# Channel attention and gated convolution on one core: taps decoded earlier, second load in two pieces, casts and transposes re-bound

## The chip, the core and the metric

The kernel runs on one core of one Trainium2 chip. The core's engines work side by side, each through its own instructions in order: TensorE (PE, with the loading of its weights shown apart as PEld), VectorE (DVE), ScalarE (ACT), GpSimd (POOL) and SyncE (SP), which issues most of the loads. The metric is the device time of one execution in microseconds (us); lower is better. It is given as the median of several runs.

## The reference

`q`, `k`, `v` are 4 x 6336 x 256 in float32 (a batch of 4, 6336 rows, 256 channels). The first half is attention over channels, the second a gated causal convolution with five taps:

```python
qn = q / (norm(q, axis=1) + 1e-6);  kn = k / (norm(k, axis=1) + 1e-6)
s = kn.transpose(0, 2, 1) @ qn / tau                 # 4 x 256 x 256
a = softmax(s)                                       # over the last axis
x = v @ a                                            # 4 x 6336 x 256
gate = sigmoid(sum_k conv_w[k] * x[:, row - 4 + k])  # five taps, causal
out = (gate * (x @ w_val)) @ w_out
```

The norms run over the 6336 rows, so a batch's scores, and with them all of its second half, are known only when all of its rows of `q` and `k` have been seen.

## The kernel before

**Two passes for each batch.** The first pass walks over `q` and `k` in 17 groups of up to 3 x 128 rows (group 0 has two such rows of 128, group 3 two and a rest of 64). A group is loaded by `load_group` (line 78) into one of six `raw` buffers, one DMA for its q and one for its k. `score_group` (line 239) adds its part to the scores: some rows go through TensorE in float32 as they are (`s_ps<-raw`), others are split into a rounded part and a remainder (`hi`: ACT's cast on line 269, POOL's subtraction on line 270) and take three faster products (`s_ps<-hi`). The squares for the norms are made on ACT (`sq`, line 288, three buffers) and added up partly on DVE in PSUM (`acc_ps`, line 293), partly on POOL (`acc`). In the first batch's groups 0 to 3 all rows go raw; from group 4 on two rows go raw and one is split. Batch 1 has raw rows only in its groups 0 to 3, and after that everything is split.

`softmax` (line 328) is a generator; each `tick` runs one stage of it: sum of both accumulators (`acc_all`, line 337), column sums on TensorE (line 342), roots, reciprocals, exponentials, `a`. Then `a` is transposed (line 395, `o_ps<-ident,a`), copied by ACT (`at`, line 399) and multiplied with w_val (line 404).

The second pass walks over `v` in 13 steps of up to 508 rows. Per step: `transpose_v` (line 436) turns `v` on TensorE (`t_ps`) and splits it (ACT line 446, DVE line 447); `conv` makes x (`x_ps`) and the tap sums (ACT line 469, DVE line 471); `sigmoid` (line 474) runs on ACT; `value` multiplies x @ w_val in (DVE line 489); `split_g` splits the product into `g_hi` (ACT line 502) and `g_lo` (POOL line 503); `finish` (line 506) multiplies by w_out (`o_ps`, line 519) and stores.

**Interleaving.** The second pass of batch b is interleaved with the first pass of batch b+1: the last loop (line 691) runs per step the steps of the one and as many groups of the other as `due_after` asks for. `split_group` issues a group's cast, squares and additions, `run_group` its products. Only batch 0's first pass runs alone.

**Inputs in 64 bits.** The weights and the taps come as 64-bit floats and are decoded with integer operations on DVE (`decode`, `decode_past`), w_val and the taps (`wk`, 10 x 128, ten operations on lines 152 to 166, 204, 206) during batch 0's first pass. The raw words of w_val lie in one of the three `hi` buffers until then.

**What sets the order.** A scheduler orders each engine's instructions after the order of the program text, priorities (`high_priority` around the softmax stages) and explicit bindings: `behind("KEY")` makes what is issued inside wait in the order, not in time, until after the instruction last marked with that key. Marks used here: `SIG` the sigmoid, `ACT` the last copy of an output pair or of a softmax stage, `VH` the cast of v, `GH` the cast to `g_hi`, `SCORES` the last score product. PSUM tiles with the tag `bank` share four banks: `o_ps`, `t_ps`, `val_ps`, the softmax's and `warm`; a tile waits until the one that had its bank has been read.

Of the kernel before, what the change touches and what calls it, by code (L numbers as in the profile page):

```python
# [17 lines left out]
P = 128  # L18
# [6 lines left out]
EARLY = 2  # L25
# [6 lines left out]
def kernel(  # L32
# [45 lines left out]
    def load_group(b, g):  # L78
        j0, n = groups[g]
        t = raw_p.tile([P, 2, GROUP, C], F32, name="raw")  # L80
        for s, src in ((0, q), (1, k)):
            main = src[b, 0:RP * P].rearrange("(p j) c -> p j c", j=RP)
            last_load[0] = nc.sync.dma_start(out=t[:, s, 0:n, :], in_=main[:, j0:j0 + n, :])  # L83
            if rest_of(g):
                nc.sync.dma_start(out=t[0:REST, s, n, :], in_=src[b, RP * P:N])
        raws[b, g] = t
# [152 lines left out]
    def score_group(b, g):  # L239
# [58 lines left out]
        with tc.issue_after(cast.ins) if cast else nullcontext():  # L298
            if owed:
                owed.pop()()  # L300
            if b == 1 and LEAD <= g < LEAD + OWE:
                owed.append(norms)
            elif not late:
                norms()
# [18 lines left out]
        if late:  # L323
            later.append(norms)
        return ([clear] if g == 0 else []) + [lambda np_=np_, j=j: mms(np_, j) for np_, j0, nj in parts for j in range(j0, j0 + nj)]


    def softmax(b):
# [64 lines left out]
        for h in range(NH):  # L393
            for h2 in range(NH):
                nc.tensor.transpose(at_ps[:, (h2 * NH + h) * P:(h2 * NH + h + 1) * P],
                                    a[:, h, h2 * P:(h2 + 1) * P], ident)
        yield
# [108 lines left out]
    def finish(b, i):  # L506
# [5 lines left out]
        for j in range(0, nt, 2):  # L512
            pair = offs[j:j + 2]
            o_ps = ps.tile([P, 512], F32, name="o_ps", tag="bank")
            for u, off in enumerate(pair):
                n_ = 0
                for h in range(NH):
                    for gs, ws in ((gh, wo_hi), (gh, wo_lo), (gl, wo_hi)):
                        nc.tensor.matmul(o_ps[:, u * C:(u + 1) * C], gs[:, h, off:off + P], ws[:, h, :],  # L519
                                         start=n_ == 0, stop=n_ == 3 * NH - 1)  # L520
                        n_ += 1
            if (b, i) == all_steps[-1]:

                for u, (copy, dma) in enumerate(((nc.scalar.copy, nc.scalar), (nc.vector.tensor_copy, nc.sync))[:len(pair)]):
                    copy(o_sb[:, j + u, :], o_ps[:, u * C:(u + 1) * C])
                    first = max((j + u) * P - pair[u], 0)
                    dma.dma_start(out=out[b, t0 + pair[u] + first:t0 + pair[u] + P], in_=o_sb[first:P, j + u, :])
                continue
# [62 lines left out]
    for n in range(NG):  # L591
        if n == 1:
            load_taps()
            load_weights(0)
            for _ in prepare_weights(2):
                pass
            prep.append(prepare_weights(0))
        if n == NG - 4:
# [7 lines left out]
        with behind(*(["SPIN"] if n < 2 else [])):  # L606
            run_group()
        if n == 0:
            with behind("SCORES"):
                spin(4)  # L610
        if n == 9:
# [79 lines left out]
    for n in range(len(all_steps)):  # L691
# [3 lines left out]
        turns = due_after(n) - (issued - len(ready))  # L695
        if n == 0:
            sigmoid(*now)
        for turn in range(turns):
            if turn == 0:
                run_group()  # L700
                with behind(*(["ACT", "VH", "SIG"] if n < EARLY else ["ACT"])):
                    split_group()
# [24 lines left out]
        if new:  # L727
            for h in range(NH):
                transpose_v(*new, h)
        tick()  # L730
# [36 lines left out]
```

## Time and profile before

| What | Value |
|---|---|
| median of 3 runs | 649.9 us (649.16 to 649.97) |
| profiled execution, its own time | 649.27 us |
| its span, first to last instruction | 647.4 us |
| PE busy | 635.9 us, 98% of the span |
| DVE, ACT, POOL busy | 523.4, 470.9, 391.3 us |
| mean granted TensorE clock | 0.995 of full speed |
| loaded and stored | 79.11 MB and 25.95 MB |

A row of the timeline reads: start, duration, engine, line, operation, output tile <- input tiles, sizes, number of merged instructions, and in square brackets the idle time of the engine before it and what ended it. "SPq" and "ACTq" are the sequencers that issue DMAs. Rows of equal instructions are merged, and durations of PE overlap (the ends of matmuls are modelled), so distances are read from start to start. PEclk is the granted clock, 1.00 is full speed.

### The profile page before, as it was taken

The page shows a single profiled execution, that of the slowest core. Times are in us where ns is not written, and L with a number is a line of the kernel's source. Part 1 is how long each engine was busy: PE and PEld are TensorE (multiplying, and loading weights), DVE is VectorE, ACT ScalarE, POOL GpSimd, SP SyncE. Part 2 cuts the span into 40 slices and gives each one's busy share as a digit, 9 for nine tenths or more (in the row PEclk, how much of TensorE's full clock was granted, in tenths as well). Part 3 has the DMA queues.
Part 4 walks back from the last instruction along what each step waited for, and adds up shares of the span by engine and source line. Part 5 has one row for each costly group of instructions (what it writes and reads, how often), then busy time and mean ns, then how long its engine had stood idle before and what let it go on. Part 6 is the DMA issues. An engine that isn't in the chain of part 4 may idle for free.

```text
span 647.4 us, 10814 instructions
## 1 busy us (share of the span) xinstructions
PE 635.9 (98%) x4051; PEld 573.0 (89%) x4051; DVE 523.4 (81%) x826; ACT 470.9 (73%) x620; POOL 391.3 (60%) x205
## 2 busy tenths in 40 slices
PE   9999999999999999999999999999999999999996
PEld 7888889999888999999998989999998898888886
DVE  4999798787787878878787869777878889888884
ACT  5677797858787697778788688778679565655564
POOL 2784599768655598859765559686775222212221
PEclk9989999999999999999999999999999999999998
DMA  8989665455434556545543546552322343343213
GB/s 299 402 294 347 207 230 172 151 191 184 128 118 146 196 177 207 181 147 174 166 159 99 190 154 223 189 170 66 97 80 67 123 132 110 106 131 107 64 41 111
DMA packets 73674, 105.77 MB, mean 163 GB/s; under 512 B 4300, under 2 KB 55702, under 8 KB 73622
## 3 DMA queue, kind: packets, MB, share of 16 engines
q1 hardware_dynamic: 47846, 79.76, 37.0%
q10 hardware_dynamic: 25776, 25.32, 12.5%
q8 instruction: 32, 0.52, 0.3%
q14 instruction: 20, 0.16, 0.1%
HBM read 79.11 MB, written 25.95 MB: 162 GB/s over the span
## 4 chain that ended last, share of the span: by engine, by line
PE 86%; DVE 5%; ACT 3%; POOL 2%; issue 1%; DMA 1%; SPq 1%; ACTq 0%; POOLq 0%
PE o_ps L519 21%; PE x_ps L455 20%; PE s_ps L316 19%; PE val_ps L455 19%; PE t_ps L445 6%; DVE gate L471 2%; DMA raw<-in_k_dram 1%; POOL hi L270 1%; PE o_ps L404 1%; DVE acc_ps L293 1%; SPq L83 0%; ACT L477 0%; ACT L375 0%; ACT sq L288 0%; POOL g_lo L503 0%
## 5 line engine op out<-in xcount | busy, mean ns | idle before, releaser
L471 DVE SCALAR_TENSOR_TENSOR gate<-x_ps,cw,gate 128x508 f32<-128x508 f32 (+1 forms) x416 | 276.6, 720 | 12.6 <-ACT gate L469 10.6
L270 POOL TENSOR_TENSOR hi<-raw,hi 128x1536 fp32r<-128x1536 f32 (+3 forms) x62 | 180.3, 2911 | 81.7 <-ACT hi L269 81.7
L503 POOL TENSOR_TENSOR g_lo<-gate,g_hi 128x1016 fp32r<-128x1016 f32 (+1 forms) x50 | 116.2, 2324 | 110.2 <-ACT g_hi L502 101.1
L293 DVE TENSOR_TENSOR acc_ps<-acc_ps,sq 128x512 f32<-128x512 f32 (+1 forms) x135 | 94.1, 697 | 71.0 <-ACT sq L288 68.6
L455 PE MATMUL x_ps<-v_hi,w 128*128 128x512 f32 (+1 forms) x416 | 140.2, 394 | 0.9 <-DVE rz L379 0.9
L316 PE MATMUL s_ps<-hi 128*128 128x256 f32 (+1 forms) x912 | 131.6, 289 | 2.8 <-POOL hi L270 2.6
L455 PE MATMUL val_ps<-v_hi,w 128*128 128x508 f32 (+1 forms) x416 | 133.8, 383 | 0.0
L316 PEld LDWEIGHTS s_ps<-hi 128*128 128x128 f32 (+1 forms) x912 | 118.6, 191 | 7.7 <-POOL hi L270 3.6
L529 ACT COPY o_sb<-o_ps 128x512 f32<-128x512 f32 x99 | 58.2, 588 | 78.3 <-PE o_ps L519 78.1
L519 PE MATMUL o_ps<-wo_hi,g_hi 128*128 128x256 f32 x400 | 113.3, 283 | 1.3 <-ACT at L399 1.3
L519 PE MATMUL o_ps<-wo_hi,g_lo 128*128 128x256 f32 x400 | 112.3, 281 | 0.0
L519 PE MATMUL o_ps<-wo_lo,g_hi 128*128 128x256 f32 x400 | 112.2, 281 | 0.0
L288 ACT ACTIVATE sq<-raw 128x1536 f32<-128x1536 f32 (+2 forms) x72 | 96.0, 1342 | 4.9 <-DVE acc_ps L293 3.9
L455 PEld LDWEIGHTS x_ps<-v_hi,w 128*128 128x128 f32 x416 | 77.4, 188 | 15.3 <-ACT z L377 1.3
L455 PEld LDWEIGHTS val_ps<-v_hi,w 128*128 128x128 f32 x416 | 77.1, 188 | 13.6
L293 POOL TENSOR_TENSOR acc<-acc,sq 128x512 f32<-128x512 f32 x57 | 74.5, 1306 | 23.2 <-ACT sq L288 23.0
L469 ACT ACTIVATE gate<-x_ps,cw 128x508 f32<-128x508 f32 (+1 forms) x104 | 68.4, 670 | 20.8 <-PE x_ps L455 20.2
L269 ACT CAST hi<-raw 128x1536 fp32r<-128x1536 f32 (+3 forms) x62 | 76.8, 1241 | 5.7 <-PE s_ps L316 2.0
L446 ACT CAST v_hi<-t_ps 128x512 fp32r<-128x512 f32 (+1 forms) x104 | 56.1, 567 | 33.9 <-PE t_ps L445 31.3
L455 PE MATMUL x_ps<-v_lo,w 128*128 128x512 f32 (+1 forms) x208 | 79.6, 382 | 0.0
L455 PE MATMUL val_ps<-v_lo,w 128*128 128x508 f32 (+1 forms) x208 | 79.1, 380 | 0.0
L489 DVE TENSOR_TENSOR gate<-val_ps,gate 128x508 f32<-128x508 f32 (+1 forms) x104 | 64.1, 658 | 17.4 <-ACT gate L477 17.2
(114 smaller groups left out, 819.4 us busy)
## 6 DMA issues: line engine op xcount, KB each, us to landing
raw<-in_q_dram SPq DMA_DIRECT2D x60, 384.0 KB
raw<-in_k_dram SPq DMA_DIRECT2D x60, 384.0 KB
v_raw<-in_v_dram SPq DMA_DIRECT2D x44, 512.0 KB
out_dram<-o_sb ACTq DMA_DIRECT2D x47, 384.0 KB
out_dram<-o_sb ACTq DMA_DIRECT2D x47, 124.0 KB
raw<-in_q_dram SPq DMA_DIRECT2D x8, 256.0 KB
raw<-in_k_dram SPq DMA_DIRECT2D x8, 256.0 KB
v_raw<-in_v_dram SPq DMA_DIRECT2D x4, 384.0 KB
```

The costliest lines, as they stand in the source:

```text
L269: cast = nc.scalar.copy(hi[r, js, :, 0, :], rows_of[r, js])
L270: nc.gpsimd.tensor_tensor(hi[r, js, :, 1, :], rows_of[r, js], hi[r, js, :, 0, :].bitcast(F32), ALU.subtract)
L288: nc.scalar.activation(sq[0:np_, ja:jb], rows_of[0:np_, ja:jb], AF.Square)
L293: add = eng.tensor_tensor(st[key][0:np_], st[key][0:np_], sq[0:np_, j], ALU.add)
L316: marks["SCORES"] = nc.tensor.matmul(st["s"][:, h, :], lhs, rhs, start=False, stop=stop and h == NH - 1 and n_ == len(ops) - 1)
L455: marks["PRODUCT"] = nc.tensor.matmul(ps, wt[:, which, ws, ch, hs], vs[:, ch, lo:hi_], start=ws == 0 and ch == 0 and vs is th, stop=ws == ...
L469: marks["TAP"] = nc.scalar.activation(gate[:, h, 0:w], x_ps[:, 0:w], AF.Copy, scale=cw[:, h:h + 1])
L471: marks["GATE"] = nc.vector.scalar_tensor_tensor(gate[:, h, 0:w], x_ps[:, tap:tap + w], cw[:, tap * NH + h:tap * NH + h + 1], gate[:, h, 0 ...
L489: nc.vector.tensor_tensor(gate[:, h, 0:w], vals[h][:, 0:w], gate[:, h, 0:w], ALU.mult)
L503: nc.gpsimd.tensor_tensor(gl[:, :, 0:w], gate[:, :, 0:w], gh[:, :, 0:w].bitcast(F32), ALU.subtract)
L519: nc.tensor.matmul(o_ps[:, u * C:(u + 1) * C], gs[:, h, off:off + P], ws[:, h, :], start=n_ == 0, stop=n_ == 3 * NH - 1)
L529: marks["ACT"] = nc.scalar.copy(o_sb[:, j:j + len(pair), :], o_ps[:, 0:len(pair) * C].rearrange("p (j c) -> p j c", c=C))
```

## The change

1. `load_group`: group 1 of batch 0 is loaded in two pieces, row block 0 first (q and k), then blocks 1 and 2. Its product list gets a `pause` of two dummy products (`spin(2)`) after the first row block; the four dummy products after group 0 are gone.
2. The taps (and tau) are loaded ahead of group 3 instead of behind group 4, and their ten decoding operations are issued at n == 0 instead of n == 1. w_val's load stays where it was.
3. The sigmoid of step 0 is issued after the step's first `run_group`, and in step 0 the cast of the next group is no longer bound behind it; the squares that batch 1's groups 4 to 6 owe to a later turn are bound behind the last sigmoid instead. From the third step on (`n >= EARLY`) a step's first cast is bound behind `GH`, the cast to `g_hi`, too.
4. The last transpose of `a` is marked `AT`, and the transposes of `v` are issued behind it.
5. In the very last step the two halves of the output pair go to two PSUM banks instead of one.

```diff
@@ load_group
-        for s, src in ((0, q), (1, k)):
-            main = src[b, 0:RP * P].rearrange("(p j) c -> p j c", j=RP)
-            last_load[0] = nc.sync.dma_start(out=t[:, s, 0:n, :], in_=main[:, j0:j0 + n, :])
-            if rest_of(g):
-                nc.sync.dma_start(out=t[0:REST, s, n, :], in_=src[b, RP * P:N])
+        for ja, jb in ((0, 1), (1, n)) if (b, g) == (0, 1) else ((0, n),):
+            for s, src in ((0, q), (1, k)):
+                main = src[b, 0:RP * P].rearrange("(p j) c -> p j c", j=RP)
+                last_load[0] = nc.sync.dma_start(out=t[:, s, ja:jb, :], in_=main[:, j0 + ja:j0 + jb, :])
+                if rest_of(g):
+                    nc.sync.dma_start(out=t[0:REST, s, n, :], in_=src[b, RP * P:N])
@@ score_group
             if owed:
-                owed.pop()()
+                with behind("SIG"):
+                    owed.pop()()
...
-        return ([clear] if g == 0 else []) + [lambda np_=np_, j=j: mms(np_, j) for np_, j0, nj in parts for j in range(j0, j0 + nj)]
+        def pause():
+            with behind("SCORES"):
+                spin(2)
+
+        products = ([clear] if g == 0 else []) + [lambda np_=np_, j=j: mms(np_, j) for np_, j0, nj in parts for j in range(j0, j0 + nj)]
+        if (b, g) == (0, 1):
+            products.insert(1, pause)
+        return products
@@ softmax
-                nc.tensor.transpose(at_ps[:, (h2 * NH + h) * P:(h2 * NH + h + 1) * P],
-                                    a[:, h, h2 * P:(h2 + 1) * P], ident)
+                marks["AT"] = nc.tensor.transpose(at_ps[:, (h2 * NH + h) * P:(h2 * NH + h + 1) * P],
+                                                  a[:, h, h2 * P:(h2 + 1) * P], ident)
@@ finish
             pair = offs[j:j + 2]
+            last = (b, i) == all_steps[-1]
             o_ps = ps.tile([P, 512], F32, name="o_ps", tag="bank")
+            halves = [o_ps, ps.tile([P, 512], F32, name="o_ps", tag="bank") if last and len(pair) > 1 else o_ps]
             for u, off in enumerate(pair):
                 n_ = 0
+                o_ps = halves[u]
...
-                    copy(o_sb[:, j + u, :], o_ps[:, u * C:(u + 1) * C])
+                    copy(o_sb[:, j + u, :], halves[u][:, u * C:(u + 1) * C])
@@ the loops
     for n in range(NG):
-        if n == 1:
+        if n == 0:
             load_taps()
-            load_weights(0)
             for _ in prepare_weights(2):
                 pass
+        if n == 1:
+            load_weights(0)
             prep.append(prepare_weights(0))
...
-        if n == 0:
-            with behind("SCORES"):
-                spin(4)
...
-        if n == 0:
-            sigmoid(*now)
         for turn in range(turns):
             if turn == 0:
                 run_group()
-                with behind(*(["ACT", "VH", "SIG"] if n < EARLY else ["ACT"])):
+                if n == 0:
+                    sigmoid(*now)
+                with behind(*(["ACT", "VH"] + ["SIG"] * (n > 0) if n < EARLY else ["ACT", "GH"])):
                     split_group()
...
         if new:
-            for h in range(NH):
-                transpose_v(*new, h)
+            with behind("AT"):
+                for h in range(NH):
+                    transpose_v(*new, h)
```

The order of POOL's instructions stays the same throughout; on the other engines the change reads as follows at three places. The line numbers of the changed kernel are a few higher.

The first place is DVE in batch 0's first pass, from the first addition of squares (`acc_ps<-acc_ps,sq`; `wk` are the taps, `bits` belongs to w_val). Before:

```order
L293 TENSOR_TENSOR acc_ps<-acc_ps,sq 128x512 x7
L152 TENSOR_SCALAR wk<-wk_raw 10x128
L293 TENSOR_TENSOR acc_ps<-acc_ps,sq 64x512
L154 SCALAR_TENSOR_TENSOR wk_raw<-wk_raw,wk 10x128
L176 TENSOR_SCALAR bits<-w_raw 128x512
L156 TENSOR_SCALAR wk<-wk_raw 10x128
L293 TENSOR_TENSOR acc_ps<-acc_ps,sq 128x512
L158 TENSOR_SCALAR wk<-wk 10x128
L293 TENSOR_TENSOR acc_ps<-acc_ps,sq 128x512
L178 SCALAR_TENSOR_TENSOR w_raw<-w_raw,bits 128x512
L160 TENSOR_SCALAR wk<-wk 10x128
L162 SCALAR_TENSOR_TENSOR wk<-wk_raw,wk 10x128
```

and now:

```order
L294 TENSOR_TENSOR acc_ps<-acc_ps,sq 128x512 x2
L153 TENSOR_SCALAR wk<-wk_raw 10x128
L294 TENSOR_TENSOR acc_ps<-acc_ps,sq 128x512
L155 SCALAR_TENSOR_TENSOR wk_raw<-wk_raw,wk 10x128
L157 TENSOR_SCALAR wk<-wk_raw 10x128
L159 TENSOR_SCALAR wk<-wk 10x128
L294 TENSOR_TENSOR acc_ps<-acc_ps,sq 128x512
L161 TENSOR_SCALAR wk<-wk 10x128
L294 TENSOR_TENSOR acc_ps<-acc_ps,sq 128x512
L163 SCALAR_TENSOR_TENSOR wk<-wk_raw,wk 10x128
L294 TENSOR_TENSOR acc_ps<-acc_ps,sq 128x512
L165 TENSOR_SCALAR wk_raw<-wk_raw 10x128
```

The first taps operation has moved from behind the seventh addition to behind the second, and the rest now stand singly or in threes between the additions of groups 1 to 3; the run of four without an addition (lines 162 to 204), which stood before group 5's additions, is gone.

The second place is ACT at the start of the second pass of batch 0, from the cast of batch 1's group 4 to the cast to `g_hi` of step 0. Before:

```order
L269 CAST hi<-raw 128x6x256
L446 CAST v_hi<-t_ps 128x512 x2
L477 ACT_TABLE_LOAD
L477 ACTIVATE gate<-gate 128x1016
L269 CAST hi<-raw 128x6x256
L288 ACTIVATE sq<-raw 128x1536
L446 CAST v_hi<-t_ps 128x512
```

and now:

```order
L270 CAST hi<-raw 128x6x256
L455 CAST v_hi<-t_ps 128x512 x2
L270 CAST hi<-raw 128x6x256
L486 ACT_TABLE_LOAD
L486 ACTIVATE gate<-gate 128x1016
L289 ACTIVATE sq<-raw 128x1536
L455 CAST v_hi<-t_ps 128x512
```

The cast of group 5 has moved ahead of the sigmoid and its table load.

The third place is TensorE in the softmax of batch 2, and the same again in batches 1 and 3 (`a` is the attention matrix, `v_raw` the next step's v). Before:

```order
L455 MATMUL x_ps<-v_hi,w 128x512
L395 MATMUL o_ps<-ident,a 128x128 x2
L445 MATMUL t_ps<-ident,v_raw 128x128 x4
L395 MATMUL o_ps<-ident,a 128x128 x2
L445 MATMUL t_ps<-ident,v_raw 128x128 x4
L519 MATMUL o_ps<-wo_hi,g_hi 128x256
```

and now:

```order
L464 MATMUL x_ps<-v_hi,w 128x512
L404 MATMUL o_ps<-ident,a 128x128 x4
L454 MATMUL t_ps<-ident,v_raw 128x128 x8
L531 MATMUL o_ps<-wo_hi,g_hi 128x256
L531 MATMUL o_ps<-wo_lo,g_hi 128x256
```

All of `a` is transposed ahead of `v`; on ACT the copy to `at` has accordingly moved ahead of both casts of `v` (it stood between them).

## The prediction

> **What bounds the kernel now.** I read the page first, then the waits of TensorE, then its timeline around each wait, and last what the releaser had been doing.
>
> ```profile
> span 647.4 us, 10814 instructions
> ```
>
> PE is busy for 98% of this span (first part of the page, in the table above), so only the few places where it waits or runs slowly can give time back. The waits name them (us in total, times, longest):
>
> ```profile
> PE s_ps L316 <- POOL hi L270: 2.6, 2, 1.4
> PE o_ps L519 <- ACT at L399: 1.3, 2, 1.0
> ```
>
> The first row's two waits are in batch 0's first pass and early in its second pass; the second row's are in the softmaxes of batches 1 and 2. The granted clock is read from windows of the first pass (the columns are PE, PEld, DVE, ACT and POOL busy, PEclk, DMA share, GB/s):
>
> ```profile
> 29.62:33.03 3.41, 2.04 (x13) 1.54 (x12) 3.34 (x6) 2.74 (x3) 3.41 (x4) 1.00 1.03 401
> 33.03:36.44 3.41, 3.41 (x9) 2.70 (x10) 3.34 (x6) 2.55 (x3) 3.41 (x3) 0.50 0.85 331
> 84.23:87.64 3.41, 2.41 (x15) 1.80 (x13) 3.41 (x7) 3.41 (x4) 3.41 (x2) 1.00 0.34 113
> ```
>
> After a window in which PE was busy for 2.04 of 3.41 us, the next 3.41 us were granted half the clock. A window with 2.41 us busy had no such sequel.
>
> **Part 1: the taps on DVE.** TensorE's timeline around that place:
>
> ```profile
> 28.39 1.89 PE L316 MATMUL s_ps<-raw 128*128 128x256 f32 x8
> ...
> 31.76 0.85 PE L316 MATMUL s_ps<-hi 128*128 128x256 f32 x5 [1.37 <-POOL hi L270]
> 32.54 0.38 PE L233 MATMUL tau_ps<-tau_sb,ones 1*128 1x1 f32 x2
> 32.85 3.64 PE L316 MATMUL s_ps<-raw 128*128 128x256 f32 x8
> ...
> 37.08 1.89 PE L316 MATMUL s_ps<-raw 128*128 128x256 f32 x8
> ...
> 39.51 1.89 PE L316 MATMUL s_ps<-raw 128*128 128x256 f32 x8
> ```
>
> An undisturbed group takes 39.51 - 37.08 = 2.43 us. The group from 28.39 took 32.85 - 28.39 = 4.46; less 2.43 and tau's 0.31 (32.54 to 32.85) the wait cost 1.7. The group at half clock took 37.08 - 32.85 = 4.23, so the slow clock cost 1.8. Why was POOL late?
>
> ```profile
> 11.61 1.27 POOL L293 TENSOR_TENSOR acc<-acc,sq 128x512 f32<-128x512 f32 x1 [10.11 <-ACT sq L288]
> ...
> 14.46 0.20 DVE L152 TENSOR_SCALAR wk<-wk_raw 10x128 int32<-10x128 int32 x1
> 14.96 1.28 POOL L270 TENSOR_TENSOR hi<-raw,hi 128x512 fp32r<-128x512 f32 x1 [2.08 <-ACT hi L269]
> ...
> 20.90 1.27 POOL L270 TENSOR_TENSOR hi<-raw,hi 128x512 fp32r<-128x512 f32 x1
> 21.05 1.27 DVE L162 SCALAR_TENSOR_TENSOR wk<-wk_raw,wk 10x128 int32<-10x128 int32 x1
> ...
> 26.86 0.68 DVE L293 TENSOR_TENSOR acc_ps<-acc_ps,sq 128x512 f32<-128x512 f32 x1
> ...
> 27.57 1.49 ACT L288 ACTIVATE sq<-raw 128x1536 f32<-128x1536 f32 x1 [3.20 <-DVE acc_ps L293]
> 28.97 0.60 ACT L269 CAST hi<-raw 128x512 fp32r<-128x512 f32 x1
> ...
> 29.37 0.69 DVE L182 TENSOR_SCALAR bits<-bits 128x512 int32<-128x512 int32 x1
> ...
> 30.45 1.26 POOL L270 TENSOR_TENSOR hi<-raw,hi 128x512 fp32r<-128x512 f32 x1
> ```
>
> A taps operation alone takes 0.20 us; one that meets a POOL instruction ends just behind it (22.32 against 22.17) and so takes up to 1.27. Four such in a row held group 5's additions back to 27.54. With three `sq` buffers group 8's squares had to wait for these, group 9's cast stood behind the squares on ACT, POOL's subtraction behind the cast, and PE behind that.
>
> In the new order the taps run from about 10.2 us on, since their load now stands right behind group 2's k (landed by 10.04, ACT's row below). I add up DVE's new order from there, additions at 0.70, taps operations at 0.3 where POOL is idle (by its two rows until 11.61 and from 12.88 to 14.96) and at POOL's next end where it is not. Depending on who wins two close races, group 4's additions end at 22.4 or 23.7 us, group 5's at 24.4 or 25.7, and the operation of row 29.37 at 27.0 or 28.3. Group 8's squares then start by 25.7, group 9's cast by 27.2, POOL's addition and subtraction end by 29.8. PE, some 0.4 us earlier than now (part 2), wants it at 29.7: the wait goes, and with it the low window and the slow clock. That is 3.5 us on PE.
>
> What is late next is DVE itself, at the end of the pass, where the norms need all sums:
>
> ```profile
> 45.21 1.43 DVE L293 TENSOR_TENSOR acc_ps<-acc_ps,sq 128x512 f32<-128x512 f32 x2 [0.15 <-ACT sq L288]
> 47.10 3.71 DVE L293 TENSOR_TENSOR acc_ps<-acc_ps,sq 128x512 f32<-128x512 f32 x5 [0.46 <-ACT sq L288]
> ...
> 51.05 0.69 DVE L337 TENSOR_TENSOR acc_all<-acc_ps,acc 128x512 f32<-128x512 f32 x1
> ...
> 51.79 0.70 PE L342 MATMUL o_ps<-acc_all,ones 128*128 128x256 f32 x2
> ```
>
> DVE has only 0.6 us of waits left in these 20 us, and an operation on w_out moves from ahead of `acc_all` to behind it (it holds about 0.3 there, the distance from 50.81, the end of the additions, to 51.05). So `acc_all`, which now ends at 51.74, can end 1.7 + 0.3 = 2.0 to 3.0 + 0.6 + 0.3 = 3.9 us earlier, while PE would be there 3.9 earlier (3.5 and part 2). Parts 1 and 2 together gain 2.0 to 3.9; I take 3.4, nearer the end at which DVE wins the races, since POOL has gaps in front of both.
>
> **Part 2: the second group in two pieces.** Its whole gain stands or falls with this start:
>
> ```profile
> 6.82 1.05 PE L103 MATMUL warm<-ones 128*128 128x128 f32 x8
> ...
> 7.91 0.63 ACT L284 ACTIVATE acc<-raw 128x512 f32<-128x512 f32 x1 [2.46 <-DMA raw<-in_k_dram]
> 7.96 10.13 PE L316 MATMUL s_ps<-raw 128*128 128x256 f32 x44
> ...
> 10.04 1.49 ACT L288 ACTIVATE sq<-raw 128x1536 f32<-128x1536 f32 x1 [0.56 <-DMA raw<-in_k_dram]
> ```
>
> A third of group 1 (256 of 768 KB) can be on hand when group 0's products end at 6.82. Its eight passes at 1.89/8 and less (0.86 together), the two dummies (half of 1.05) and the other two row blocks (1.73) end at 9.9; group 2 may start when its k lands, at 10.04 and a little. Now group 1 would end at 7.96 + 12 x 0.216 = 10.55 (0.216 is the pass distance in the row of 44). Gain 0.4; nothing if the first piece lands no earlier than 7.8, 0.5 if group 2 lands earlier. Two DMA issues more on SP, and the taps' and tau's two moved ahead of group 3, delay group 3's and 4's issues; both hide under what is queued already, as PE now reaches group 3 near 13 us. Uncovered they would cost up to an issue each, some 0.4.
>
> **Part 3: sigmoid and casts.** Early in the second pass:
>
> ```profile
> 74.68 1.05 ACT L477 ACTIVATE gate<-gate 128x1016 f32<-128x1016 f32 x1 [1.12 <-DVE gate L471]
> 75.64 1.47 ACT L269 CAST hi<-raw 128x1536 fp32r<-128x1536 f32 x1
> ...
> 77.19 3.53 POOL L270 TENSOR_TENSOR hi<-raw,hi 128x1536 fp32r<-128x1536 f32 x1 [2.31 <-ACT hi L269]
> ...
> 84.27 3.53 POOL L270 TENSOR_TENSOR hi<-raw,hi 128x1536 fp32r<-128x1536 f32 x1
> ...
> 87.84 2.29 PE L316 MATMUL s_ps<-hi 128*128 128x256 f32 x17 [1.20 <-POOL hi L270]
> ```
>
> The cast of row 75.64 moves ahead of table load and sigmoid, which start 0.35 later, in place of the 1.12 us that ACT idled. POOL need not idle its 2.31; what follows on POOL (an addition, `g_lo`, the subtraction of row 84.27) then hangs on ACT, 0.7 earlier than now, and on `g_lo`. POOL's last subtraction ends 1.4 to 1.7 us earlier, and PE's wait of 1.20 goes: 1.2, at least 0.5 if the sigmoid's delay is passed on to `g_hi`, at most 1.4 with its tail. The binding behind `GH` moves nothing in later steps, so it costs nothing.
>
> **Part 4: a ahead of v.** In batch 2:
>
> ```profile
> 346.61 0.58 ACT L446 CAST v_hi<-t_ps 128x512 fp32r<-128x512 f32 x1
> 347.08 0.60 ACT L399 COPY at<-o_ps 128x512 f32<-128x512 f32 x1
> ...
> 347.73 0.39 PE L519 MATMUL o_ps<-wo_hi,g_hi 128*128 128x256 f32 x1 [1.00 <-ACT at L399]
> ```
>
> PE waits for the bank that `at` empties. With `at` first in place of `v_hi` it comes 0.47 earlier (347.08 - 346.61). In batch 1 the wait is only 0.3 (1.3 - 1.0 in the waits) and goes; in batch 3 the waits show none. Sum 0.8. What is late next is the copy of the first output pair, now behind both casts of v; it gives back up to 0.3 in batch 2. Bounds 0.4 and 1.2 (the rest of both waits and 0.2 at their ends).
>
> **Part 5: a bank for each last half.**
>
> ```profile
> 642.49 0.42 DVE L525 COPY o_sb<-o_ps 128x256 f32<-128x256 f32 x1 [2.27 <-ACT o_sb L525]
> 642.95 0.33 SPq L527 DMA_DIRECT2D out_dram<-o_sb  x1
> ```
>
> DVE's copy would start beside ACT's, 0.4 us earlier. But 4.45 us of the span follow the last issue, in which the stores issued before it drain on the same engines; I take 0.1, from 0 to 0.4.
>
> **The sum.** 3.4 + 1.2 + 0.8 + 0.1 = 5.5 us. In the profiled execution the span would be 641.9, and its own time, 649.27 with 1.87 us around the span, 643.8. That execution lay 0.6 us below the median of the runs (649.9), so the median should be 644.4. Behind part 3 PE is starved at few places, so what it gains by then it keeps.
>
> By the Trainium skill, "TensorE: Matmul & The Clock Gate", section "Why this matters for your kernels", the clock falls back only after idle gaps of about 3 us; here a gap of 1.37 us was followed by half the clock, so this trace disagrees. By that rule the slow stretch would not hang on the wait, would stay, and the sum would be 3.7 in place of 5.5.
>
> **The rivals.** *DVE stays late.* The taps meet POOL everywhere or load later, and the wait near 30 us survives in part with its slow clock. For it: six of the ten still come behind POOL's row at 14.96. Against it: three or four now fall into POOL's gaps before it. Parts 1 and 2 then give only about 0.8; 649.9 - 0.8 - 2.1 = 647.0.
>
> *The slow clock stays.* Some other low window brings half the clock although the wait is gone, or it never hung on the wait. For it: 2.04 and 2.41 us of busy time lie close on either side of the turn. Against it: the stretch came exactly one window after the wait and nowhere else. 644.4 + 1.8 = 646.2.
>
> *DVE blocks on the taps' landing: slower.* Lines 153 and 155 now stand between the two additions of group 1 and hold everything behind them. Row 14.46 does not tell when the taps landed, only that it was by then. Did they land at 14.4 in the new order too, seven minus two additions (3.5 us) would be queued behind them, DVE would be 3.5 us later than now at that point, and PE would wait that much in groups 8 and 9, with a second slow stretch of 1.8: +5.3 - 1.7 (what the new order spares) - 2.1 (parts 3 to 5) = 1.5, 651.4. It decides from a landing about 3 us later than the 10.2 I assume; against it speaks that the load's place in SP's queue moves ahead of six DMAs.
>
> *Nothing moves.* Each wait is replaced by one as long on the next engine: 649.9. Against it: ACT and POOL have idle time at every one of these places.
>
> **How the numbers follow.** Forecast 0.68, own range 642.8 to 646. DVE late 0.14, slow clock 0.05, slower 0.06, nothing 0.07. Below 642.3 lie all upper bounds together (3.9 + 1.4 + 1.2 + 0.4 = 6.9 gives 643.0) and a run of the faster kind. The range 642.3 to 648.2 leaves out the slower rival, nothing and a little at the lower end. About 0.2% (1.3 us) can be told from no change: faster by more 0.85, within it 0.09, slower by more 0.06.
>
> **What would show it.** Right: no wait of PE near 30 us, granted clock 1.00 in every window from 6 us to the end of the matmuls, `acc_all` ended by 49 us; no PE wait for `hi` near 82 us; `at` ahead of both `v_hi`, and no PE wait at `o_ps` over 0.6 us; DVE's last copy starting with ACT's. Wrong: a DVE wait for a DMA near 10 us of more than 2 us, a window of half clock after 10 us, PE waiting for `acc_all` by over 2 us, or a new PE wait over 1 us between 60 and 110 us.

## The result, and the profile after

The changed kernel takes 643.89 us (median of 5 runs, 642.97 to 643.94) beside 649.47 before (649.16 to 649.97): a ratio of 0.9909, 95% interval 0.9895 to 0.9924. The forecast was 644.4, range 642.3 to 648.2. The sum came out well, but its parts did not come out as forecast.

TensorE's waits in the changed kernel (us in total, times, longest):

```profile
PE x_ps L464 <- DVE rz L388: 0.9, 1, 0.9
PE o_ps L531 <- ACT at L408: 0.5, 1, 0.5
PE s_ps L318 <- DMA raw<-in_k_dram: 0.5, 1, 0.5
PE s_ps L318 <- ACT hi L270: 0.2, 1, 0.2
```

Both waits for POOL's `hi` are gone, the waits for `at` have fallen from 1.3 us in two to 0.5 in one (batch 2), and a wait for a load is new. The same three windows as before (columns as in the prediction) are full, at the full clock:

```profile
29.62:33.03 3.41, 3.41 (x20) 2.99 (x19) 3.34 (x7) 2.98 (x4) 3.41 (x4) 1.00 1.03 398
33.03:36.44 3.41, 3.41 (x21) 3.10 (x20) 2.92 (x5) 2.47 (x3) 2.58 (x3) 1.00 1.04 403
84.23:87.64 3.41, 3.41 (x25) 3.15 (x24) 3.24 (x6) 3.08 (x6) 3.41 (x2) 1.00 0.99 338
```

Where the time came from is read from four points on TensorE: the first split product (group 4), the first product of the norms, the last product, the end of the span. Timeline of TensorE after, with the new wait in its second row:

```profile
17.40 1.06 PE L318 MATMUL s_ps<-hi 128*128 128x256 f32 x6
18.91 1.97 PE L318 MATMUL s_ps<-raw 128*128 128x256 f32 x8 [0.45 <-DMA raw<-in_k_dram]
...
49.22 0.60 PE L351 MATMUL o_ps<-acc_all,ones 128*128 128x256 f32 x2
...
636.24 0.40 PE L531 MATMUL o_ps<-wo_hi,g_lo 128*128 128x256 f32 x2
```

The two of these points before that the prediction does not show:

```profile
17.73 1.06 PE L316 MATMUL s_ps<-hi 128*128 128x256 f32 x6
...
641.77 0.28 PE L519 MATMUL o_ps<-wo_hi,g_lo 128*128 128x256 f32 x1
```

| stretch | before, us | after, us | gained | forecast |
|---|---|---|---|---|
| start to the first split product | 17.73 | 17.40 | 0.33 | 0.4 (part 2) |
| to the norms' product | 34.06 | 31.82 | 2.24 | 3.0 (part 1, bounded by DVE) |
| to the last product's end | 590.26 | 587.42 | 2.84 | 2.0 (parts 3 and 4) |
| to the end of the span | 5.35 | 5.56 | -0.21 | 0.1 (part 5) |
| sum | 647.4 | 642.2 | 5.2 | 5.5 |

DVE, which had set the end of the first pass, has `acc_all` ready well before TensorE asks for it at 49.22:

```profile
46.98 0.69 DVE L346 TENSOR_TENSOR acc_all<-acc_ps,acc 128x512 f32<-128x512 f32 x1 [0.18 <-POOL acc L294]
```

It ends at 47.67, 4.07 us earlier than before (51.74).

### The profile page after: what moved, and what is told of

Read it like the earlier page. It is cut to its first block, busy times and chain, and to the rows that moved or that the text cites. A ratio compares the mean times of both kernels' runs of the same rounds, so it can differ in the third digit from the quotient of the medians.

```text
span 642.2 us, 10808 instructions
## 1 busy us (share of the span) xinstructions
PE 633.5 (99%) x4047; PEld 571.8 (89%) x4047; DVE 518.6 (81%) x826; ACT 470.5 (73%) x620; POOL 391.4 (61%) x205
## 4 chain that ended last, share of the span: by engine, by line
PE 93%; DMA 2%; ACT 1%; DVE 1%; SPq 1%; issue 1%; ACTq 0%
PE s_ps L318 22%; PE o_ps L531 21%; PE x_ps L464 21%; PE val_ps L464 20%; PE t_ps L454 7%; DMA raw<-in_k_dram 2%; PE o_ps L413 1%; DVE gate L480 1%; SPq L84 1%; PE o_ps L351 0%; ACT hi L270 0%; PE o_ps L404 0%; DVE gate L498 0%; ACT gate L478 0%; PE o_ps L353 0%
```

## Experiments

**Part 1 alone**, on the kernel before:

```diff
-        if n == 1:
+        if n == 0:
             load_taps()
-            load_weights(0)
             for _ in prepare_weights(2):
                 pass
+        if n == 1:
+            load_weights(0)
```

> The kernel before with part 1 alone (the taps' load and their ten operations among the first groups, the load of w_val one group later than they). Theory of the prediction: the wait of TensorE near 30 us and the half clock behind it go together and DVE does not become the bound, so TensorE gains 3.3 to 3.6 us, acc_all ends by 48.5 us, no window after 8 us has less than the full clock, and the time is 646.0 to 646.3 beside 649.5 before. Rival one, the gain of the whole change near 30 us needed part 2 as well: the wait near 30 us is cut to between 0.4 and 1.0 us and the time is 647.5 or more. Rival two, on the wait for group 5's k that the changed kernel has at 18.5 us: if the taps' place ahead of group 3 makes that load late, TensorE waits for a load between 17 and 20 us here too; if the two pieces of group 1 make it late, there is no such wait here.

Measured: 646.62 us (646.21 to 647.46), ratio 0.9953 (0.9938 to 0.9967), above the 646.0 to 646.3 expected. There is no wait of TensorE near 30 us. TensorE's first split product, its wait for group 5's k, and the norms' product:

```profile
18.15 1.06 PE L316 MATMUL s_ps<-hi 128*128 128x256 f32 x6
19.77 2.00 PE L316 MATMUL s_ps<-raw 128*128 128x256 f32 x8 [0.56 <-DMA raw<-in_k_dram]
...
50.11 0.60 PE L342 MATMUL o_ps<-acc_all,ones 128*128 128x256 f32 x2
```

From 18.15 to 50.11 it took 31.96 us, 2.10 less than before, not the 3.3 to 3.6 expected. The wait for the load is there although group 1 comes in one piece here. So part 1 carries about half of the whole gain, and the late load of group 5 is its doing.

**The wait filled** (called fill below). The kernel before with the same wait near 30 us, but with dummy products in it:

```diff
+        def fill():
+            with behind("SCORES"):
+                spin(6)
...
+        if (b, g) == (0, 9):
+            def last(f=products[2]):
+                with behind("SPIN"):
+                    f()
+            products[2:] = [fill, last]
```

> The kernel before with six dummy products (about 1.3 us) on TensorE ahead of group 9's split products: the wait near 30 us stays as long as it is, but TensorE is busy in it. If the half clock hangs on the low window, as the prediction has it, the window after it is granted 1.00, group 10 takes 2.4 us in place of 4.2, and the time falls by 1.8, to 647.7 beside 649.5. If the slow clock has another cause (rival: the slow clock stays), a window of half clock follows all the same and the time is 649.4 to 649.8.

Measured: 650.34 us (649.48 to 650.75, 10 runs), ratio 1.0011 (1.0001 to 1.0020). No gain, although the stretch of half clock is not in its profile. The windows of fill:

```profile
29.63:33.04 3.41, 3.33 (x25) 2.90 (x23) 3.34 (x7) 2.74 (x4) 3.41 (x3) 1.00 1.03 400
33.04:36.45 3.41, 3.41 (x20) 3.11 (x21) 3.34 (x7) 3.35 (x4) 3.41 (x4) 1.00 1.00 378
```

TensorE runs on at full clock, waits 0.5 us for POOL's `hi` near 45 us, where it had not waited before, and then stands before DVE's sum (timelines of DVE and TensorE in fill):

```profile
51.60 0.68 DVE L154 SCALAR_TENSOR_TENSOR w_raw<-w_raw,wb 128x512 int32<-128x512 int32 x1
52.20 0.68 DVE L347 TENSOR_TENSOR acc_all<-acc_ps,acc 128x512 f32<-128x512 f32 x1
...
52.93 0.70 PE L352 MATMUL o_ps<-acc_all,ones 128*128 128x256 f32 x2 [1.32 <-DVE acc_all L347]
```

DVE's chain does not depend on how TensorE fares here: up to 50 us its operations stand about 0.4 later than in the kernel before, as they already did at 26 us, ahead of the wait. One operation on w_out (0.6 us) has slipped ahead of `acc_all`; without it TensorE would still have waited 0.7. So in the kernel before, the wait and the half clock were time that TensorE would have spent waiting for DVE anyway. Part 1 could pay only because DVE's chain became shorter too.

The runs of the kernel before beside the experiments say the same of the clock. A window of 3.41 us at half takes 0.0026 from the mean granted clock of a span of 647.4 us, which leaves 0.997 at most. Of 35 runs 27 had 0.998 or more, so no such window; 8 had 0.995, as the profiled one, and are taken to have had it. Their medians are 649.55 and 649.57 us.

**Two small loads ahead of group 3**, on the kernel before, to find why group 5 comes late:

```diff
+        if n == 0:
+            for s in range(2):
+                nc.sync.dma_start(out=const.tile([1, 1], F32, name=f"spare{s}"), in_=tau)
         if n == 1:
             load_taps()
```

> The kernel before, its taps where they were, with two more loads of four bytes each (tau into two spare cells that nothing reads) ahead of group 3 on SP. Theory of the eight places: the two places alone delay groups 3 and 4 as in the changed kernel, the k of group 4 is issued after 9.5 us (before: 7.84), the stretch from 9 to 16 us carries 280 to 330 GB/s on the mean (before: 333 and 392), and the k of group 5 lands at 18.3 us or later (before: 17.47); the time is 649.5 to 650.2. Rival, the ten rows of the taps or their place ahead of the groups' rows slow the transfers: here all stays as before, k of group 4 by 8.2 us, group 5's k by 17.9 us, and 649.5.

**The taps' and tau's loads on ACT**, on the changed kernel, the opposite trial:

```diff
-        nc.sync.dma_start(out=raw.rearrange("p n o -> p (n o)"), in_=src.rearrange("k (h n) -> (k h) n", h=NH))
-        nc.sync.dma_start(out=tau_sb, in_=tau)
+        nc.scalar.dma_start(out=raw.rearrange("p n o -> p (n o)"), in_=src.rearrange("k (h n) -> (k h) n", h=NH))
+        nc.scalar.dma_start(out=tau_sb, in_=tau)
```

> The changed kernel with the taps' and tau's loads issued by ACT instead of SP, all else as it is. Theory: SP has a ring of eight loads and issues a load only when the one eight places ahead has landed whole; the two small loads ahead of group 3 take two of the eight places, so groups 3 and 4 are issued about 2 us later (the changed kernel's k of group 4 at 10.1 us, before at 7.8) and the transfer engines run short between 9 and 16 us (about 300 GB/s where before had 333 and 392). Then here the k of group 4 is issued by 8.0 us, 9 to 16 us carry over 330 and over 380 GB/s, group 5's k lands by 17.9 us, TensorE has no wait for a load after 9 us, and the time is 643.2 to 643.5 beside 643.9. Rival: the shortage is chance or comes from the order of the decode, or from the taps' transfer itself; then the two windows stay near 300 GB/s, TensorE waits 0.3 to 0.6 us for group 5's k near 18.5 us, and the time stays at 643.9.

Results of the two trials together. The windows from 9 to 16 us (last columns: PEclk, DMA share, GB/s), in the kernel before:

```profile
9.15:12.56 3.41, 3.41 (x17) 3.00 (x16) 2.37 (x4) 2.35 (x3) 0.95 (x1) 1.00 1.06 333
12.56:15.97 3.41, 3.41 (x16) 2.57 (x14) 3.25 (x6) 2.76 (x4) 1.33 (x2) 1.00 1.04 392
```

With the two small loads:

```profile
9.15:12.56 3.41, 3.41 (x18) 3.00 (x17) 1.69 (x3) 2.68 (x4) 0.24 (x1) 1.00 0.94 296
12.56:15.97 3.41, 3.41 (x17) 2.74 (x16) 3.24 (x7) 2.84 (x4) 1.71 (x2) 1.00 0.89 309
```

In the changed kernel:

```profile
9.15:12.56 3.41, 3.41 (x18) 2.91 (x17) 2.92 (x8) 2.40 (x3) 0.83 (x1) 1.00 1.01 318
12.56:15.97 3.41, 3.41 (x16) 2.49 (x15) 3.41 (x7) 2.91 (x4) 1.60 (x2) 1.00 0.96 303
```

With the taps' and tau's loads on ACT:

```profile
9.15:12.56 3.41, 2.80 (x13) 2.17 (x13) 1.45 (x3) 2.33 (x2) 0.00 (x0) 1.00 1.04 334
12.56:15.97 3.41, 3.41 (x17) 2.74 (x16) 3.13 (x5) 2.49 (x4) 1.49 (x2) 1.00 1.04 392
```

SP's issue of group 4's k, from SP's timeline of the kernel before:

```profile
7.84 0.33 SPq L83 DMA_DIRECT2D raw<-in_k_dram  x1
```

With the two small loads:

```profile
10.69 0.33 SPq L83 DMA_DIRECT2D raw<-in_k_dram  x1
```

In the changed kernel:

```profile
10.09 0.33 SPq L84 DMA_DIRECT2D raw<-in_k_dram  x1
```

With the loads on ACT:

```profile
8.36 0.33 SPq L84 DMA_DIRECT2D raw<-in_k_dram  x1
```

Two loads of four bytes each are enough to hold group 4's k back from 7.84 to 10.69 us and to cut the traffic to 300 GB/s. With the loads on ACT the traffic is back, and the issue nearly so (8.36, where 8.0 was expected). In the trace each issue follows the landing of the load eight places before it: 7.82 for the issue at 7.84, 10.67 for 10.69, 10.08 for 10.09. So the small loads cost places, not bytes. The trace also shows what the places are: the program uses eight semaphores (counters that tell of a landing) for these loads in turn, and a load is issued when the earlier load on its semaphore has landed. The two loads on ACT use two of the same eight; but ACT issues them at 0.73 and 1.43 us, and they have landed by 2.5 us, ahead of SP's next loads on these two at 3.61 and 5.04. Whether issuing them first from SP would do as well was not tried. The kernel with the two small loads took 650.50 us (649.06 to 650.78, 10 runs), ratio 1.0010 (1.0001 to 1.0019). Its profile, too, has neither the wait near 30 us nor the half clock, and TensorE waits for `acc_all` instead:

```profile
51.59 0.70 PE L342 MATMUL o_ps<-acc_all,ones 128*128 128x256 f32 x2 [0.57 <-DVE acc_all L337]
```

With the loads on ACT the time was 643.97 (643.70 to 644.20), ratio 0.9914 (0.9899 to 0.9929), no better than the changed kernel's and outside the 643.2 to 643.5 expected, although the stretch from the first split product to the norms' product was now 30.68 us, 1.14 less than changed. It had lost 1.1 us in waits for groups 1 and 2. Whether that is chance is tried below.

**w_val two groups later**, on the changed kernel:

```diff
-        if n == 1:
+        if n == 3:
             load_weights(0)
             prep.append(prepare_weights(0))
...
-        if n >= 3:
+        if n >= 6:
             for gen in prep:
```

> The changed kernel with the load of w_val behind group 6 instead of ahead of group 5, and its decode begun three groups later. If the late load of group 5 (its k lands at 18.8 us) is only a matter of bytes queued ahead of it, it lands 1.3 us earlier (512 KB at 400 GB/s), TensorE's wait of 0.4 us at 18.5 us goes and with it the cost behind it, and the time is 643.2 to 643.5 beside 643.9. Rival: DVE now has the decode of w_val closer to the end of the pass, acc_all ends later than 48.5 us (the changed kernel: 47.7) and TensorE waits for it; then 643.9 to 645.

Measured: 646.01 us (645.06 to 647.34), ratio 0.9945 (0.9928 to 0.9963), slower than changed. The wait for group 5 went, and from the first split group (18.15) to the last (47.93) TensorE took 29.78 us, where the changed kernel took 30.92 (17.40 to 48.32). But with the decode later on DVE, `acc_all` ends at 50.30 in place of 47.67, and the norms' product comes at 51.73 in place of 49.22. It does not wait for `acc_all` there: TensorE's order has changed, and batch 1's first products, with a wait of 0.7 us for ACT's copy of the scores (`s`), now stand ahead of it. The first x behind the softmax waits as well (waits of TensorE here):

```profile
PE x_ps L464 <- DVE w L398: 1.7, 1, 1.7
...
PE s_ps L323 <- ACT s L348: 0.7, 1, 0.7
```

The rival that the expectation named has the place right (DVE late at the end of the pass), but not the wait, and its 643.9 to 645 was too low.

**One piece or two, and the spread of the head** (the head is the time up to the first split product). Part 2 undone in the changed kernel, and in the one with the loads on ACT; beside the latter, both of its neighbours once more on the same chip:

```diff
-        for ja, jb in ((0, 1), (1, n)) if (b, g) == (0, 1) else ((0, n),):
+        for ja, jb in ((0, n),):
...
-        if (b, g) == (0, 1):
-            products.insert(1, pause)
...
+        if n == 0:
+            with behind("SCORES"):
+                spin(4)
```

> The changed kernel with part 2 undone: group 1 loaded in one piece, four dummies after group 0 in place of two after the first piece. Prediction: part 2 is worth 0.4 us, so this kernel takes 644.3 beside 643.9. Rival, formed from the changed kernel's trace: the pieces cost more than they bring, since group 5's k lands 1.3 us later than before and TensorE waits for it at 18.5 us; then that load lands near 17.5 us here, no wait stands at 18.5 us, and the time is 643.0 to 643.4. Second rival: the late load has nothing to do with the pieces (chance, or the taps' place in the queue); then the wait at 18.5 us is here too and the time is 644.2 or more.

> The changed kernel once more, to stand beside the next three. From the traces so far the arrival of groups 1 and 2 differs from one execution to the next (the k of group 2 landed between 9.8 and 12.0 us in kernels that load them alike). If that is chance, the start of the first split products falls anywhere from 17.2 to 19.3 us here, the part from there to TensorE's last product is again 619.2 (within 0.3, given the wait for group 5's k), and the time is 643.9 within 0.5. If the first execution was a lucky one, the time is 644.5 or more.

> The kernel with the taps' and tau's loads on ACT once more. Behind the start of the first split products it took 618.15 us to TensorE's last product, 1.1 less than the changed kernel, but it had waited 1.0 us for groups 1 and 2. If these waits were chance, the kernel is 0.4 to 1.0 us faster than the changed kernel on the same chip. Rival: the loads that are now issued earlier share the transfer engines with groups 1 and 2 and make them late each time; then waits of 0.3 to 0.6 us for them are here again and the time is equal within 0.3.

> The kernel with the taps' and tau's loads on ACT, and part 2 undone (group 1 in one piece, four dummies after group 0). Prediction of part 2: it is worth 0.4 us, so this kernel takes 0.4 more than the one with two pieces on the same chip. Rival one: what group 1's products gain is lost in waiting for group 2, whose loads land when they did, so the difference is under 0.2. Rival two: the pieces cost, because two more loads take places of the eight; then this kernel is 0.2 to 0.8 faster.

| kernel | median, us | range | ratio to before, 95% interval | first split product | to the norms' product |
|---|---|---|---|---|---|
| one piece, loads on SP | 644.42 | 643.62 to 644.81 | 0.9916 (0.9901 to 0.9930) | 17.61 | 31.43 |
| changed, again | 644.22 | 644.08 to 645.31 | 0.9923 (0.9909 to 0.9937) | 18.76 | 31.70 |
| two pieces, loads on ACT, again | 643.30 | 643.06 to 643.97 | 0.9907 (0.9894 to 0.9921) | 18.49 | 30.68 |
| one piece, loads on ACT | 643.17 | 642.69 to 643.67 | 0.9904 (0.9890 to 0.9917) | 17.32 | 30.67 |

The last three stood on one chip. One piece with the loads on SP settles what makes group 5 late: TensorE's waits view names no wait for it there, but ACT's cast of it still waits for the load until 18.67 us (changed: 18.85), and the stretch to the norms is 31.43 us, 0.8 more than with the loads on ACT. So the pieces are not the cause. Only part of the loss is one visible wait: in the changed kernel the products of group 5 start 0.6 us late, and 0.5 more is lost in groups 5 to 7, most of it where weight loads of split products wait for POOL's `hi` (0.20 and 0.29 us).

The changed kernel's own repeat shows what the head does by chance: its first split product came 1.36 us later than in the first execution, after waits for loads, and its profiled time was 1.3 us longer (645.21 and 643.93); the rest, from there to the last product's end, was 619.15 against 619.24. The row of its waits for loads:

```profile
PE s_ps L318 <- DMA raw<-in_k_dram: 2.1, 3, 1.5
```

With the loads on ACT the stretch is 30.68 us again, 1.0 less than changed on that chip, and the time 0.9 less; there, too, TensorE waited for group 2 (1.2 us). With the first executions on other chips taken in, the medians are 643.8 (8 runs) and 644.0 (10 runs). The gain in the stretch is steady: 30.67 or 30.68 in all three profiles with the loads on ACT, 31.16 to 31.96 in the seven with the taps' loads on SP ahead of group 3 and w_val's in its place. How much of it is seen in the time is up to the head. One piece in place of two differs by 0.13, within the spread. Over all fourteen profiled executions the first split product comes at 17.18 to 19.28 us with two pieces (eight) and at 17.32 to 18.49 with one (six). Part 2 is worth nothing that these runs can show (less than about 0.5 either way). The kernel with one piece and the loads on ACT is the fastest of all: 1.05 us less than changed on the same chip, with ranges that do not touch, though the intervals of the two ratios overlap by 0.0008. TensorE's first split product and the norms' product in it:

```profile
17.32 1.06 PE L318 MATMUL s_ps<-hi 128*128 128x256 f32 x6
...
47.99 0.60 PE L349 MATMUL o_ps<-acc_all,ones 128*128 128x256 f32 x2
```

Its waits hold no load:

```profile
PE x_ps L462 <- DVE rz L386: 0.9, 1, 0.9
PE o_ps L529 <- ACT at L406: 0.5, 1, 0.5
PE s_ps L318 <- ACT hi L270: 0.2, 1, 0.2
```

**Part 3 undone**, in the changed kernel:

```diff
+        if n == 0:
+            sigmoid(*now)
         for turn in range(turns):
             if turn == 0:
                 run_group()
-                if n == 0:
-                    sigmoid(*now)
-                with behind(*(["ACT", "VH"] + ["SIG"] * (n > 0) if n < EARLY else ["ACT", "GH"])):
+                with behind(*(["ACT", "VH", "SIG"] if n < EARLY else ["ACT"])):
...
-                with behind("SIG"):
-                    owed.pop()()
+                owed.pop()()
```

> The changed kernel with part 3 undone (the sigmoid of the first step ahead of the cast, no binding of the norms behind it). Prediction: part 3 is worth 1.2 us by its wait alone, and 1.5 by the distance between the products' starts in the two traces, so the wait of TensorE for POOL's subtraction is back near 82 us with 1.0 to 1.4 us, and the time is 645.1 to 645.5 beside 643.9. Rival: the wait went because everything ahead of it came earlier (parts 1 and 2), not by the order of sigmoid and cast; then no wait over 0.3 us is back and the time stays within 0.3 us of 643.9.

Measured: 645.67 us (645.20 to 646.73), ratio 0.9939 (0.9924 to 0.9954). The wait is back as it was (TensorE's timeline, part 3 undone):

```profile
50.44 0.60 PE L350 MATMUL o_ps<-acc_all,ones 128*128 128x256 f32 x2
...
86.36 2.29 PE L317 MATMUL s_ps<-hi 128*128 128x256 f32 x17 [1.21 <-POOL hi L271]
...
639.02 0.40 PE L530 MATMUL o_ps<-wo_hi,g_lo 128*128 128x256 f32 x2
```

From the norms' product to the end of the last it takes 588.98 us, the changed kernel 587.42: the part is worth 1.56 us. In the changed kernel POOL does the two subtractions in one go, with no idle time between them:

```profile
68.65 7.01 POOL L271 TENSOR_TENSOR hi<-raw,hi 128x1536 fp32r<-128x1536 f32 x2 [4.82 <-ACT hi L270]
```

**Part 4 undone**, in the changed kernel:

```diff
-            with behind("AT"):
-                for h in range(NH):
-                    transpose_v(*new, h)
+            for h in range(NH):
+                transpose_v(*new, h)
```

> The changed kernel with part 4 undone (the transposes of v not bound behind those of a). Prediction: part 4 is worth 0.8 us (0.4 to 1.2), 0.5 of it in batch 2, 0.3 in batch 1 and none in batch 3: TensorE's waits for at are 1.0 us near 345 us and 0.3 near 187 us, and the time is 644.5 to 644.9 beside 643.9. From the starts of the products in the two traces the part is worth 1.1, with 0.3 in batch 3 as well: then about 645.0. Rival: the bank was freed earlier by other parts; no wait over 0.6 us is back and the time stays within 0.3 us.

Measured: 645.08 us (644.32 to 645.87), ratio 0.9931 (0.9916 to 0.9946). The waits for `at` are back, 1.3 us in two. TensorE's timeline without part 4: the norms' product, the products on `at` in batches 1 and 2, the last product:

```profile
48.59 0.60 PE L351 MATMUL o_ps<-acc_all,ones 128*128 128x256 f32 x2
...
187.98 1.89 PE L413 MATMUL o_ps<-wa,at 128*128 128x256 f32 x8
...
344.41 1.89 PE L413 MATMUL o_ps<-wa,at 128*128 128x256 f32 x8
...
636.78 0.40 PE L531 MATMUL o_ps<-wo_hi,g_lo 128*128 128x256 f32 x2
```

The same products in the changed kernel:

```profile
188.09 1.93 PE L413 MATMUL o_ps<-wa,at 128*128 128x256 f32 x8
...
344.03 1.94 PE L413 MATMUL o_ps<-wa,at 128*128 128x256 f32 x8
```

From the norms' product to the last product's end it is 588.59 against 587.42: 1.17 us. From the norms' product to batch 1's row 139.39 against 138.87 (0.52), from there to batch 2's 156.43 against 155.94 (0.49); what is left, 0.16, comes behind batch 2, where the waits view names no wait for `at`.

**Part 5 undone**, in the changed kernel:

```diff
-            halves = [o_ps, ps.tile([P, 512], F32, name="o_ps", tag="bank") if last and len(pair) > 1 else o_ps]
+            halves = [o_ps, o_ps]
```

> The changed kernel with part 5 undone (both halves of the last pair in one bank). Prediction: the part is worth 0.1 us (0 to 0.4), DVE's last copy starts 0.4 later against TensorE's end, and the time is 644.0 beside 643.9. By the traces so far the stretch from TensorE's last product to the end of the span was 5.35 us before and 5.57 after, so the part is worth nothing: the stretch here is 5.3 to 5.5 us. Were it worth its whole 0.4 us, the stretch here would be 5.9 or more.

Measured: 643.71 us (642.33 to 643.98), ratio 0.9908 (0.9894 to 0.9921), beside 644.22 for the changed kernel on that chip, within the spread of the head. The span ends 5.5 us after TensorE's last product with one bank and 5.5 and 5.6 with two, although DVE's copy does start earlier with two. The last product and DVE's copy with one bank, then DVE's copy and its store in the changed kernel:

```profile
635.93 0.28 PE L531 MATMUL o_ps<-wo_hi,g_lo 128*128 128x256 f32 x1
...
636.65 0.42 DVE L537 COPY o_sb<-o_ps 128x256 f32<-128x256 f32 x1 [2.28 <-ACT o_sb L537]
```

```profile
636.67 0.42 DVE L537 COPY o_sb<-o_ps 128x256 f32<-128x256 f32 x1 [1.89 <-PE o_ps L531]
637.12 0.33 SPq L539 DMA_DIRECT2D out_dram<-o_sb  x1
```

The copy starts 0.44 us after the last product's end with one bank, 0.03 with two. The span then ends 5.1 us after the last store's issue, against 4.45 before: the end of the span did not follow that store.

## Why the prediction was right, and where it was wrong

**Part 1: right size, half of the reason.** The wait near 30 us went, and DVE no longer binds. But the step "the wait goes, and with it the low window and the slow clock. That is 3.5 us on PE" named time that was worth nothing by itself: fill and the two small loads each have a profile without the half clock, the latter without the wait too, and both are slower than before. In the kernel before, TensorE's last split product of the pass and `acc_all` end together (51.7 us; the norms' product starts at 51.79), so both chains had to become shorter, and the gain is the smaller of the two. The step next to it said so: "What is late next is DVE itself". In the 27 of 35 runs without the slow stretch, it follows, DVE was not late next but late first. `acc_all` came 4.07 earlier, a little past the upper bound of 3.9, and TensorE, with no load in the way, took 30.67 us instead of 34.06 to the norms, 3.39 less, close to its 3.5; so TensorE bounds the pass again. That the forecast had 3.4 for parts 1 and 2 is luck: 0.4 of it was to come from part 2.

**The places on SP: the step that failed.** "Both hide under what is queued already" is refuted, and so is its price if uncovered, "some 0.4". Group 4's k was issued 2.25 us later, TensorE met group 5's k late, and of the 3.39 us 1.15 were lost in the profiled execution; on one chip the whole kernel took 0.9 more than with the loads elsewhere. The prediction had counted the issues' own durations and not what SP waits for before it issues.

**Part 2** was forecast at 0.4 and shows 0.33 in the two profiled executions, but the head moves by more than that from one execution to the next, and the comparison on one chip gives 0.13 for the other side. Not shown. (Its "eight passes" of the first piece are four: 0.86 is 4 x 0.216.)

**Part 3** was mis-sized: 1.56 instead of 1.2. The mechanism is as told: cast ahead of sigmoid, POOL without its pause, wait gone. The prediction took the gap of 1.20 for the cost, although its own first example cost 1.7 with a gap of 1.37. Here too a wait costs about 0.35 more than its gap.

**Part 4** was mis-sized: 1.17 instead of 0.8, inside its bounds of 0.4 and 1.2. Batch 2 gave 0.49, as forecast with 0.47; batch 1 gave 0.52 for a gap of 0.3, and 0.16 came behind batch 2, where nothing was counted. The give-back of up to 0.3 by the late copy of the first output pair did not show.

**Part 5** gave nothing. Its mechanism, the earlier copy, is there. The reason given against it, that the end hangs on stores issued before, fits the rows above but was not tried by itself.

So 0.8 too much for parts 1 and 2 and 0.3 too much for part 5 met 0.8 too little for parts 3 and 4; that the sum came within 0.3 us of the forecast is luck to that extent. Of the rivals, *DVE blocks on the taps' landing* is excluded (no wait of DVE for a load in the changed kernel near 10 us), and so are *DVE stays late* (`acc_all` ends at 47.67), *The slow clock stays* (no half clock between the head and the last product) and *Nothing moves*. Of the signs named in advance all the right ones came and none of the wrong ones; the wait for group 5's load was on neither list.

**The clock.** The prediction read from one execution that a window with 2.04 us busy brings half the clock after it. The kernel with w_val later has a lower window, with a gap of 1.74 us, and no half clock behind it:

```profile
62.53:65.95 3.42, 1.68 (x8) 1.07 (x7) 3.25 (x4) 1.95 (x4) 2.80 (x2) 1.00 0.98 334
65.95:69.36 3.41, 3.41 (x20) 2.90 (x19) 2.15 (x4) 1.62 (x3) 0.37 (x1) 1.00 0.83 314
```

Together with the 27 of 35 runs without the stretch, the rule that the prediction drew is not borne out, and fill does not prove it either. The Trainium skill, "TensorE: Matmul & The Clock Gate", section "Why this matters for your kernels", lets the clock fall back only after gaps of about 3 us; these windows agree with it, and the profiled execution of the kernel before remains the exception. What brought its half clock about stays open. By that rule the prediction's sum would have been 3.7; the time came out near 5.5 all the same, since the slow clock by itself had cost the kernel before nothing.

## What to carry to other kernels

Before a wait is priced, ask whether the engine that waits would only arrive earlier at the next thing that is late: a wait filled with dummy work shows it in one run. Count a small load as a whole place where loads are issued in turn behind earlier ones. If the large ones behind it are soon wanted, let it land before they need its place, as here from ACT at the start. A wait's cost is read from the starts of the products around it, not from the gap alone.

## What the runs showed of the hardware that was not expected

- SP's next load was issued 0.01 to 0.02 us after the landing of the load eight places before it (7.82 and 7.84, 10.67 and 10.69, 10.08 and 10.09), both on the same one of eight semaphores, so this wait is the program's; two loads of four bytes ahead of group 3 cut the traffic between 9 and 16 us from 333 and 392 GB/s to 296 and 309.
- The landing of the first groups varies by more than most of the parts are worth: the same program had its first split product at 17.40 and 18.76 us. From the norms' product on, executions of the kernels that keep parts 3 and 4 agree within 0.1 us (587.4 to 587.5 to the end of the last product).
- By their mean clock, 8 of 35 runs of the kernel before had a stretch at half clock like the profiled one, and it made no difference to their time (medians 649.57 and 649.55 us).
